# Adaptive-LayerNorm linear attention and Mish block in fp32: Q of two blocks as seven block products, and a new order of the steps around them

## The chip, the cores and the metric

The kernel runs on one core of a Trainium2 chip. A core has a matmul engine (TensorE, PE below), three engines for elementwise work (VectorE or DVE, ScalarE or ACT, GpSimd or POOL), and SyncE (SP), whose queue here only starts DMA transfers; POOL starts some too. Every engine works through a queue of its own in the order in which the program emitted it, and waits on semaphores for the others. The metric is the device time of one execution in microseconds (us), taken as the median over runs.

## The reference, cut to what matters

`x` is 2048 rows of 512, all data is fp32. The hidden width is F = 1792, there are 32 heads of 16, and `c` is one row, so that the six modulation vectors are the same for all rows.

```
mod = silu(c) @ w_mod                         # sa, ca, ga, sb, cb, gb, 512 each
h   = layernorm(x) * (1 + ca) + sa
q, k, v = split(h @ wqkv)                     # wqkv: 512 x 1536
phi(t)  = where(t > 0, t + 1, exp(t)) + 1e-6
kv  = phi(k)^T v   per head                   # 16 x 16
z   = sum over rows of phi(k)
o   = phi(q) kv / (phi(q) . z + 1e-6)
x   = x + ga * (o @ wo)
h   = layernorm(x) * (1 + cb) + sb
x   = x + gb * (mish(h @ w1 + b1) @ w2)
```

## The kernel before, in words

**Tiles.** The rows are four blocks (NB = 4) of 512, each of four row tiles of 128. An fp32 product is made of three fp32r products: `split` (L71) makes of a tile a high part (a copy on ACT) and a low part (a subtraction on DVE), and `mm3` (L65) issues high x high, high x low and low x high. One Q unit, a 128 x 512 output over four contraction steps, is thus 12 matmuls. Almost all SBUF tiles are 512 wide and share one pool of slots; PSUM has eight banks in three tags (`acc` 4, `h` 3, `tp` 1).

**Order.** The order is written out by hand: the order of emission is the order of each engine's queue. Work beside the matmuls lives in generators: `spawn` starts one, and each `tick()` advances all that run by one step. Moving a `spawn` or a `tick` thus moves instructions in the queues of DVE, ACT, POOL and SP relative to those of PE.

**Attention.** For each block `k_unit(b, t)` (L259) makes K of a row tile, with `phi` (L242: exp and relu on ACT, the min and sum `ku` on DVE) and a split. `g_unit(b, t)` (L271) accumulates `gacc`, the normalized x transposed times phi(k), over all rows in four PSUM banks; its operand is the split `xn` (L266) of a row tile. `transpose` (L226) makes the modulated, transposed `hf` and its split `hT`, which K and Q multiply. After the last block, `z_unit` (L280) gives the sums, and the denominators' weights follow from them on DVE (`zs`, `hmask`).

Then comes the Q phase. `q_unit(b, g)` (L288) makes Q, transposed, 128 outputs for the 512 rows of a block, and `phi` on it. `attend(b, wait)` (L683) multiplies phi(q) by the z weights (`den`, on the single `tp` bank), takes the reciprocal on DVE, sends it to DRAM and reads it back spread over partitions (`rd`, four loads on POOL's queue), lets `wait` ticks pass, and then makes `q * rd` and its split `qs`. `kv_ps` and `m_ps` fold kv and wo into one matrix `m`; `o_unit(b, t)` (L726) multiplies `qs` by `m`, and adds the residual on DVE. Before the change the order is: Q of block 0; one unit of block 1; `den` of block 0; `kv_ps`; the rest of block 1; `m_ps`; Q of block 2 with `attend(1, 4)` spawned; `o_unit(0, 0..3)` with `attend(2, 5)` spawned; `norm_sums(0)` (L733, the second LayerNorm's sums) spawned; Q of block 3.

**Second part.** The FFN's first product works on two blocks of rows at once by the Winograd form of Strassen's scheme: seven block products and 15 additions in place of eight products. For a pair `g` of hidden tiles, `pair_begin` (L947), `pair_early` (L963), `pair_middle` (L972) and `pair_end` (L979) issue the products `a11 b11`, `a12 b21`, `s1 t1`, `s2 t2`, `s3 t3`, `a22 t4` and `s4 b22`; partial sums stay in a PSUM bank and are copied to SBUF on ACT as `u1`, `u2`, `u3` (L950, L968, L975) while more is accumulated onto them. `rows(...)` prepares the sums of w1 for a pair: loads on SP, four half-width operations on DVE (L600 to L603), four splits. `two_pairs` (L1001) interleaves the first two pairs, with two functions `between` called inside; the second of them, `trail`, issues `d_unit` (L914), the FFN's second product, of an earlier hidden tile.

Of the kernel before, what the change touches and what calls it, by code (L numbers as in the profile page):

```python
# [13 lines left out]
P = 128  # L14
# [11 lines left out]
def block_kernel(ctx: ExitStack, tc: tile.TileContext, x, wqkv, wo, w1, b1t, w2, c, wmodt, out):  # L26
# [18 lines left out]
    def f32(t):  # L45
        return t.bitcast(F32)
# [3 lines left out]
    def spawn(gen):  # L50
        fresh.append(iter(gen))
# [169 lines left out]
    def sums_shift(key, b, t, sums):  # L221
        dve.tensor_tensor(nb[key, b][:, t:t + 1], sums[:, 0:1], rs[key, b][:, t:t + 1], op=ALU.mult)

    xn, hT, wq, wk = {}, {}, {}, {}

    def transpose(key, b, j, sc0, sh0, ptag, hi_engine=act):  # L226

        p = ps(ptag, f"tp_{key}_{b}_{j}")
        for t in range(4):
            pe.transpose(p[:, P * t:P * (t + 1)], xt[key, b, t][:, P * j:P * (j + 1)], ident)  # L230

        def post():
            hf = sb(f"hf_{key}_{b}_{j}")
            act.activation(hf, p, AF.Identity, bias=mc[:, sh0 + j:sh0 + j + 1], scale=mc[:, sc0 + j:sc0 + j + 1])
            yield from split(f"hT_{key}_{b}_{j}", hf, hT, (key, b, j), hi_engine=hi_engine)

        return post()
# [50 lines left out]
    def q_unit(b, g):  # L288
        p = ps("h", f"pq_{b}_{g}")
        gs = slice(P * g, P * (g + 1))  # L290
        for k in range(4):
            mm3(p, [w[:, gs] for w in wq[k]], hT["x", b, k], k == 0, k == 3)
        pq[b, g] = sb(f"q_{b}_{g}")
        spawn(phi(p, f"q_{b}_{g}", pq[b, g]))

    bc = {}

# [98 lines left out]
    for k in range(4):  # L396
        hi, lo = sb(f"hT_x_0_{k}h", F32R), sb(f"hT_x_0_{k}l", F32R)
        hT["x", 0, k] = hi, lo

        for dst, piece in [(hi, half_) for half_ in ((0, 256), (256, 512))] + [(tp0[k], (0, 512))] if k == 0 else \  # L400
                [(hi, (0, 512)), (tp0[k], (0, 512))]:
            cs = slice(*piece)
            act.activation(dst[:, cs], tp0[k][:, cs], AF.Identity, bias=mc[:, k:k + 1], scale=mc[:, 4 + k:5 + k])
        if k < 3:
            run(split(f"wk_{k + 1}", wraw[1, k + 1], wk, k + 1, pool, pool))
        if k == 0:
            act.preload_act_table_set("exp_and_others")
            mod_pair(1)
        if k == 1:
            step(xsplit[0])  # L410
            mod_col(7, sc_bc)
            plus_one(7, 8)
        if k == 3:
            step(xsplit[0])
        dve.tensor_tensor(lo, tp0[k], f32(hi), op=ALU.subtract)
        if k == 0:
            mod_pair(2)
        if k == 1:
            mod_col(3, sc_bc)
        if k < 2:  # L420
            for t in range(4):
                pe.matmul(kp[t], hi[:, tss[t]], wk[k][0], start=k == 0, stop=False)
            for st, mv_ in (hi, wk[k][1]), (lo, wk[k][0]):
                for t in range(4):
                    pe.matmul(kp[t], st[:, tss[t]], mv_, start=False, stop=False)
        if k == 0:
            tp0.append(ps("acc", "tp_x_0_3"))
            transposes_0(3, tp0[3])
# [211 lines left out]
    for b in range(1, NB):  # L640
        last = b == NB - 1
        if b == NB - 2:
            spawn(mod_side(range(8, 12), 1))
        for t in range(4):
            k_unit(b, t)
            if b + 2 < NB:
                load_x(b + 2, t)
            if last:
                load_wqkv(0, t)
                xn_split(b, t)  # L650
            elif t >= 2:
                xn_split(b, t - 2)
            tick()
        if b + 2 < NB:
            spawn(ln_side(b + 2))
        if last:
            spawn(wo_scale())
        for t in range(4):
            if not last and t % 2 == 0:
                for j in (t, t + 1):  # L660
                    tr = transpose("x", b + 1, j, 4, 0, "tp" if j == t else "h")
                    next(tr)
                    spawn(tr)
# [155 lines left out]
            if k % 2:  # L819
                yield  # L820

    for g in range(4):
        q_unit(0, g)
        load_x(1, g, "r")
        if g == 1:
            spawn(kv_side())
            spawn(mod_side([20, 21, 22, 23, 16, 17, 18, 19], 2))
        if g == 2:
            next(early_rows[0])
        tick()  # L830
    q_unit(1, 0)
    load_x(2, 0, "r")
    tick()
    run(early_rows[0])
    next(early_rows[1])
    attending = attend(0, 5)
    next(attending)
    kvs = {}
    kv_ps = ps("acc", "kv_ps")
    for g in range(4):  # L840
        for k in range(4):
            for j in range(2):
                cs = slice(P * g + 64 * j, P * g + 64 * (j + 1))
                pe.matmul(kv_ps[64 * j:64 * (j + 1), cs], wv[k][:, cs], zs[k][:, cs], start=k == 0, stop=k == 3)
    for j in range(2):
        js = slice(64 * j, 64 * (j + 1))
        dve.tensor_tensor(kv.rearrange("p (g m) -> p g m", g=4)[js, :, js],
                          kv_ps.rearrange("p (g m) -> p g m", g=4)[js, :, js],
                          bmask[js, js].unsqueeze(1).to_broadcast([64, 4, 64]), op=ALU.mult)
    spawn(split("kv", kv, kvs, 0))  # L850
    next(attending)
    spawn(attending)
    for g in range(1, 4):
        q_unit(1, g)
        load_x(2, g, "r")
        tick()
    for g in range(4):
        m_ps = ps("acc", f"m_ps_{g}")
# [1 line left out]
        spawn(split(f"m_{g}", m_ps, ms, g))  # L860
    run(early_rows[1])
    for g in range(4):
        q_unit(2, g)
        if g == 1:
            spawn(attend(1, 4))
            spawn(mod_side(range(12, 16), 1))
        load_x(3, g, "r")
        tick()
    for t in range(4):
        o_unit(0, t)  # L870
        if t == 1:
            spawn(attend(2, 5))
        tick()
    spawn(norm_sums(0))
    for g in range(4):
        q_unit(3, g)
        tick()
    act.preload_act_table_set("mish")

    order = {8: [(0, 0), (0, 2)], 9: [(0, 1)], 10: [(0, 3), (1, 0)], 11: [(1, 2)], 12: [(1, 1)], 13: [(1, 3)]}  # L880
# [95 lines left out]
        add(c22, pc, u3)  # L976
        spawn(later(c22, 2 * g + 1, 1))

    def pair_end(c0, g, pa, pc, u2):  # L979
        c12 = sb(f"c12_{g}")  # L980
        m = mish(product(g, "a22", "t4", onto=pa), c0, 2 * g + 1)
        next(m)
        spawn(m)
        product(g, "s4", "b22", onto=pc)
        add(c12, pc, u2)
        spawn(later(c12, 2 * g, 1))
        tick()

    def pair_unit(c0, g, odd, between):
        begun = pair_begin(c0, g, ("tp" if odd else "h", "h"))  # L990
# [307 lines left out]
```

## Time and profile before

| | us |
|---|---|
| median of 3 runs | 502.73 |
| lowest, highest | 500.97, 503.97 |
| the profiled execution | 502.79 |
| its span, first to last instruction | 501.0 |

Granted TensorE clock over the span: 0.997 of full.

| engine | busy us | share of the span | instructions |
|---|---|---|---|
| PE | 491.8 | 98% | 2652 |
| DVE | 349.7 | 70% | 679 |
| ACT | 289.8 | 58% | 517 |
| POOL | 143.2 | 29% | 246 |

How to read the profile's rows. A row of the timeline gives start and length in us, engine, source line, operation, out<-in by the program's names with buffer numbers left out, partitions x elements, and in brackets how long the engine had been idle and what it waited for. "x32" says that so many instructions are shown as one row. Matmuls are pipelined: their rows overlap, and the distance from start to start is what one costs. The granted clock is the share of full speed that the throttle gave TensorE. The profile is of one execution, so a sum of its durations is made against that execution's own time.

### The profile page before, as it was taken

The numbers are of one execution on the slowest core, as the hardware profiler recorded it, in microseconds if no ns is written. First come the engines' busy times: TensorE is split into PE (matmuls) and PEld (weight loads), VectorE is DVE, ScalarE is ACT, GpSimd is POOL, SyncE is SP. The second block draws the span as 40 slices with busy tenths as digits, with TensorE's granted clock in tenths as the row PEclk, the third lists the DMA queues.
The fourth block names the chain that finished last, engine by engine and source line by source line (L and its number), as shares of the span: only waits on it lengthen the run. The fifth ranks groups of instructions, "written<-read, shape, count | busy, mean of one in ns | idle before, by whom it ended". The sixth has DMA issues, their size and how long they took to land.

```text
span 501.0 us, 7672 instructions
## 1 busy us (share of the span) xinstructions
PE 491.8 (98%) x2652; PEld 414.9 (83%) x2652; DVE 349.7 (70%) x679; ACT 289.8 (58%) x517; POOL 143.2 (29%) x246
## 2 busy tenths in 40 slices
PE   7999999999999999997999999999999999999997
PEld 6788888878878888886888888888788888899997
DVE  6885664869996679956566864679953755559772
ACT  6877684735461979557568646278354555568100
POOL 3473120000212323123034311424465031545200
PEclk9999999999999999998999999999999999999999
DMA  8724754373464307419999945999999352688512
GB/s 305 284 66 88 191 126 98 100 259 106 101 182 124 96 25 254 148 42 359 329 367 314 366 144 195 298 374 324 374 379 268 83 154 84 163 216 233 125 44 85
DMA packets 66765, 98.58 MB, mean 197 GB/s; under 512 B 7405, under 2 KB 31861, under 8 KB 66726
## 3 DMA queue, kind: packets, MB, share of 16 engines
q0 software_dynamic: 29360, 45.31, 32.9%
q1 hardware_dynamic: 37220, 52.51, 32.0%
q8 instruction: 21, 0.34, 0.3%
q10 hardware_dynamic: 146, 0.26, 0.1%
q14 instruction: 18, 0.15, 0.1%
HBM read 62.92 MB, written 33.03 MB: 192 GB/s over the span
## 4 chain that ended last, share of the span: by engine, by line
PE 93%; ACT 4%; DVE 2%; DMA 1%; issue 0%; ACTq 0%
PE p_a L940 18%; PE p_s L940 7%; PE oacc L69 5%; PE oacc L68 5%; PE oacc L67 5%; PE m L69 5%; PE m L68 5%; PE m L67 5%; PE pq L67 3%; PE o L67 3%; PE gacc L68 3%; PE gacc L69 3%; PE o L69 3%; PE gacc L67 3%; PE pq L68 3%; PE o L68 3%
## 5 line engine op out<-in xcount | busy, mean ns | idle before, releaser
L945 DVE TENSOR_TENSOR c<-p_s,u 128x512 f32<-128x512 f32 x28 | 19.4, 691 | 69.2 <-ACT u L975 58.7
L968 ACT ACTIVATE u<-p_a 128x512 f32<-128x512 f32 x12 | 7.2, 599 | 31.1 <-PE p_a L940 31.1
L932 ACT ACTIVATE ub<-c,b1c 128x512 f32<-128x512 f32 x28 | 20.0, 716 | 3.6 <-DVE c L945 3.5
L1198 POOL DMA_DIRECT2D wt_m<-w2t x20 | 14.0, 703 | 25.9 <-PE m L69 17.2
L248 DVE SCALAR_TENSOR_TENSOR ku<-e_k,relu_k 128x512 f32<-128x512 f32 x16 | 11.0, 689 | 14.6 <-ACT relu_k L246 14.6
L796 ACT ACTIVATE hf_n<-tp_n,mc 128x512 f32<-128x512 f32 x16 | 11.7, 769 | 13.4 <-PE tp_n L794 13.4
L192 POOL TENSOR_TENSOR rs_n<-rs_n,half 128x1 f32<-128x1 f32 x16 | 9.6, 604 | 30.7 <-DVE rs_n L218 15.0
L950 ACT ACTIVATE u<-p_a 128x512 f32<-128x512 f32 x14 | 8.3, 596 | 16.7 <-PE p_a L940 16.7
L245 ACT ACTIVATE e_k<-pk 128x512 f32<-128x512 f32 x16 | 9.6, 598 | 13.3 <-PE pk L69 13.2
L245 ACT ACTIVATE e_q<-pq 128x512 f32<-128x512 f32 x16 | 9.4, 589 | 12.7 <-PE pq L69 12.7
L975 ACT ACTIVATE u<-p_a 128x512 f32<-128x512 f32 x14 | 8.3, 594 | 13.0 <-PE p_a L940 13.0
L587 POOL DMA_DIRECT2D w2b<-w2d x20 | 10.6, 550 | 18.1 <-DMA out_dram<-r 5.7
L945 DVE TENSOR_TENSOR c<-p_a,u 128x512 f32<-128x512 f32 x14 | 9.5, 687 | 6.2 <-PE p_a L940 2.7
L695 POOL DMA_DIRECT2D rden_d<-rden x3 | 2.2, 717 | 41.0 <-DVE rden L693 40.8
L192 POOL TENSOR_TENSOR rs_x<-rs_x,half 128x1 f32<-128x1 f32 (+1 forms) x10 | 7.4, 744 | 22.4 <-DVE rs_x L187 21.6
L581 POOL DMA_DIRECT2D wb<-w2d x14 | 9.9, 710 | 13.1 <-PE m L69 8.4
L201 ACT ACTIVATE x<-x,nb_x,rs_x 128x512 f32<-128x512 f32 x15 | 11.5, 810 | 3.6 <-DVE nb_x L196 3.1
L248 DVE SCALAR_TENSOR_TENSOR q<-e_q,relu_q 128x512 f32<-128x512 f32 x16 | 11.0, 687 | 3.4 <-ACT relu_q L246 3.4
L707 DVE SCALAR_TENSOR_TENSOR q<-q,rd 128x512 f32<-128x512 f32 x16 | 10.6, 688 | 3.2 <-DMA rd<-rden_d 3.2
L783 POOL DMA_DIRECT2D nd<-r x8 | 4.6, 571 | 27.7 <-ACT r L201 26.2
L909 ACT ACTIVATE u<-p_a,b1c 128x512 f32<-128x512 f32 x14 | 9.5, 681 | 5.1 <-PE p_a L940 5.1
L719 DVE TENSOR_TENSOR r<-o,r 128x512 f32<-128x512 f32 x16 | 10.8, 678 | 2.3 <-PE o L69 2.3
(1460 smaller groups left out, 1949.2 us busy)
## 6 DMA issues: line engine op xcount, KB each, us to landing
wm<-in_wmodt_dram SPq DMA_DIRECT2D x24, 256.0 KB, 4.6
w2b<-w2d POOLq DMA_DIRECT2D x20, 256.0 KB, 6.6
wt_m<-w2t POOLq DMA_DIRECT2D x20, 256.0 KB, 3.6
r<-in_x_dram SPq DMA_DIRECT2D x16, 256.0 KB, 3.0
x<-in_x_dram SPq DMA_DIRECT2D x15, 256.0 KB, 4.8
w1p<-in_w_dram SPq DMA_DIRECT2D x14, 256.0 KB, 4.5
w2r<-in_w_dram SPq DMA_DIRECT2D x14, 256.0 KB, 3.9
wb<-w2d POOLq DMA_DIRECT2D x14, 256.0 KB, 4.5
```

Of the source, the lines that this page charges most:

```text
L67: pe.matmul(o, st[0], mv[0], start=start, stop=False)
L68: pe.matmul(o, st[0], mv[1], start=False, stop=False)
L69: pe.matmul(o, st[1], mv[0], start=False, stop=stop)
L192: pool.tensor_tensor(y, y, half[:, lo:hi], op=ALU.pow)
L201: act.activation(dst, t, AF.Identity, bias=nb[key, b][:, j:j + 1], scale=rs[key, b][:, j:j + 1])
L245: act.activation(e, p, AF.Exp)
L248: dve.scalar_tensor_tensor(dst, e, 1.0, r, op0=ALU.min, op1=ALU.add)
L796: act.activation(hf[b, j], p, AF.Identity, bias=mc[:, 12 + j:13 + j], scale=mc[:, 16 + j:17 + j])
L932: act.activation(u, p, AF.Mish, bias=b1c[:, f:f + 1])
L940: pe.matmul(p, st, mv, start=onto is None and c == 0 and i == 0, stop=c == 1 and i == 2, skip_group_check=onto is not None)
L945: dve.tensor_tensor(out, p, u, op=ALU.add)
L1198: pool.dma_start(v, w2t[g][:, :, SUM[name], :])
```

## The change

1. Q of blocks 0 and 1 is made as a 2 x 2 block product in the same Winograd form. `q_left` makes the four weight sums of a half of the contraction, `q_right` the four sums and differences of the transposed rows `hf`, both on DVE and with splits; `q_product` issues 6 matmuls; `q_sevens` issues 2 x 7 products with their copies on ACT and six additions `cq` on DVE. The Q weights are loaded one block earlier, and `hf` of blocks 0 and 1 is kept, for block 0 as a tile in SBUF.
2. `q_right` is spawned in blocks 1 and 2 of the K phase, `q_left` in block 2, and `early_rows[0]`, which is `rows(0)`, in block 3 in place of the Q phase.
3. The new order of the Q phase: `q_sevens`; `kv_ps`; `den` of block 0; Q of block 2; `m_ps`; two Q units of block 3; `o_unit(0, 0..3)`; `norm_sums(0)` spawned; the last two Q units. `attend(0, 4)` takes the place of `attend(0, 5)`.
4. In `two_pairs` the tick at the end of the first `pair_end` goes, and so does, for the first two pairs, the tick between. `rows(2, 3)` is spawned earlier, before `o_unit(3, 3)`.

The diff, cut to its core:

```diff
+    def q_left(c):
+        a11, a21, a12, a22 = [wraw[0, k][:, h:h + 256] for k in (c, c + 2) for h in (0, 256)]
+        s12, s34 = sb(f"qs12_{c}"), sb(f"qs34_{c}")
+        s1, s2, s3, s4 = s12[:, 0:256], s12[:, 256:512], s34[:, 0:256], s34[:, 256:512]
+        dve.tensor_tensor(s1, a21, a22, op=ALU.add)
+        dve.tensor_tensor(s2, s1, a11, op=ALU.subtract)
+        dve.tensor_tensor(s3, a11, a21, op=ALU.subtract)
+        dve.tensor_tensor(s4, a12, s2, op=ALU.subtract)
+        yield
+        for n, t in (12, s12), (34, s34):
+            yield from split(f"qs{n}_{c}", t, qa, (n, c))
+
+    def q_right(c):
+        b11, b12, b21, b22 = [hfx.pop((b, k)) for k in (c, c + 2) for b in (0, 1)]
+        t = [sb(f"qt_{c}_{i}") for i in range(4)]
+        for n, (d, u, v) in enumerate(((t[0], b12, b11), (t[1], b22, t[0]), (t[2], b22, b12), (t[3], b21, t[1]))):
+            dve.tensor_tensor(d, u, v, op=ALU.subtract)
+            if n % 2:
+                yield
+        for i in range(4):
+            yield from split(f"qt_{c}_{i}", t[i], qb, (f"t{i + 1}", c))
...
+    def q_sevens(side):
...
+        for o in range(2):
+            pa[o] = q_product(o, "a11", "b11", "h")
+            u1[o] = copy(pa[o], f"qu1_{o}")
+        side(0)
+        for o in range(2):
+            p = q_product(o, "a12", "b21", ("h", "tp")[o])
+            result(0, o, p, u1[o])
+            q_product(o, "s2", "t2", onto=pa[o])
+            u2[o] = copy(pa[o], f"qu2_{o}")
+            side(1 + o)
+        for o in range(2):
+            pc[o] = q_product(o, "s1", "t1", ("h", "acc")[o])
+            q_product(o, "s3", "t3", onto=pa[o])
+            u3[o] = copy(pa[o], f"qu3_{o}")
+            result(1, 2 + o, pc[o], u3[o])
+            side(3 + o)
+        for o in range(2):
+            result(0, 2 + o, q_product(o, "a22", "t4", onto=pa[o]), None)
+        side(5)
+        for o in range(2):
+            q_product(o, "s4", "b22", onto=pc[o])
+            result(1, o, pc[o], u2[o])
+        side(6)
...
             k_unit(b, t)
...
+            if b == NB - 2:
+                load_wqkv(0, t)
+                if t == 1:
+                    spawn(q_right(1))
+            if last and t == 0:
+                spawn(early_rows[0])
             if last:
-                load_wqkv(0, t)
...
             g_unit(b, t)
+            if b == 1 and t == 1:
+                spawn(q_right(0))
+            if b == 2 and t < 2:
+                spawn(q_left(t))
...
-    for g in range(4):
-        q_unit(0, g)
...
-    q_unit(1, 0)
...
+    q_sevens(beside_q)
+    load_x(2, 3, "r")
     next(early_rows[1])
...
-    for g in range(1, 4):
-        q_unit(1, g)
-        load_x(2, g, "r")
+    for g in range(4):
+        q_unit(2, g)
+        if g == 1:
+            spawn(attend(1, 4))
+            spawn(mod_side(range(12, 16), 1))
+        load_x(3, g, "r")
         tick()
...
     run(early_rows[1])
     for g in range(4):
-        q_unit(2, g)
...
-    for t in range(4):
-        o_unit(0, t)
...
-    spawn(norm_sums(0))
-    for g in range(4):
-        q_unit(3, g)
-        tick()
+        q_unit(3, g)
+        tick()
         if g == 1:
+            for t in range(4):
+                o_unit(0, t)
+                if t == 1:
+                    spawn(attend(2, 5))
+                tick()
+            spawn(norm_sums(0))
...
-    def pair_end(c0, g, pa, pc, u2):
+    def pair_end(c0, g, pa, pc, u2, step=True):
...
-        tick()
+        if step:
+            tick()
...
-        pair_end(c0, g0, *s0)
+        pair_end(c0, g0, *s0, step=False)
...
     for t in (2, 3):
+        if t == 3:
+            spawn(rows(2, 3))
         o_unit(NB - 1, t)
         tick()
...
         if g == 1:
-            spawn(rows(2, 3))
             norm_next()
-            two_pairs(0, 0, 1, begun, (tick, trail(0, rows(3, 2))))
+            two_pairs(0, 0, 1, begun, (lambda: None, trail(0, rows(3, 2))))
```

More of the change, by code (lines that the diff above doesn't have):

```diff
@@ new lines, in q_right, with q_product @@
+    def q_right(c):
[7 more added lines that the diff above has]
+            yield from split(f"qt_{c}_{i}", t[i], qb, (f"t{i + 1}", c))
+    def q_product(o, left, right, tag=None, onto=None):
+        p = onto if onto is not None else ps(tag, f"pq_{left}_{o}")
+        for c in range(2):
+            if left[0] == "a":
+                st, lo = wq[c + 2 * (left != "a11")], 256 * (left == "a22") + P * o
+            else:
+                n = int(left[1])
+                st, lo = qa[(12, 12, 34, 34)[n - 1], c], 256 * ((n - 1) % 2) + P * o
+            mv_ = qb[right, c] if right[0] == "t" else hT["x", int(right[2]) - 1, c + 2 * (right[1] == "2")]
+            st = [h[:, lo:lo + P] for h in st]
+            for i, (l, r) in enumerate(((st[0], mv_[0]), (st[0], mv_[1]), (st[1], mv_[0]))):
+                pe.matmul(p, l, r, start=onto is None and c == 0 and i == 0, stop=c == 1 and i == 2,
+                          skip_group_check=onto is not None)
+        return p
@@ new lines, in q_sevens, with result, copy @@
+    def q_sevens(side):
+        pa, pc, u1, u2, u3 = {}, {}, {}, {}, {}
+        def result(b, g, p, u):
+            if u is not None:
+                c = sb(f"cq_{b}_{g}")
+                dve.tensor_tensor(c, p, u, op=ALU.add)
+                p = c
+            pq[b, g] = sb(f"q_{b}_{g}")
+            spawn(phi(p, f"q_{b}_{g}", pq[b, g]))
+        def copy(p, name):
+            u = sb(name)
+            act.activation(u, p, AF.Copy)
+            return u
+        for o in range(2):
[21 more added lines that the diff above has]
+        side(6)
@@ L398, in block_kernel @@
         hT["x", 0, k] = hi, lo
[L400 to L401 removed]
+        hf_k = hfx[0, k] = sb(f"hf_x_0_{k}")
+        for dst, piece in [(hi, half_) for half_ in ((0, 256), (256, 512))] + [(hf_k, (0, 512))] if k == 0 else \
+                [(hi, (0, 512)), (hf_k, (0, 512))]:
             cs = slice(*piece)
@@ L844, in block_kernel @@
                 pe.matmul(kv_ps[64 * j:64 * (j + 1), cs], wv[k][:, cs], zs[k][:, cs], start=k == 0, stop=k == 3)
+    attending = attend(0, 4)
+    next(attending)
+    next(attending)
     for j in range(2):
```

31 lines of the change are left out of this document (12 added, 19 removed).

## The prediction

> **What bounds the kernel now.** I read the first part of the profile's page, then the chain of work that ended last, then the waits of TensorE (PE), and only then stretches of the timeline.
>
> ```profile
> span 501.0 us, 7672 instructions
> ...
> PE 491.8 (98%) x2652; PEld 414.9 (83%) x2652; DVE 349.7 (70%) x679; ACT 289.8 (58%) x517; POOL 143.2 (29%) x246
> ...
> PE 93%; ACT 4%; DVE 2%; DMA 1%; issue 0%; ACTq 0%
> ```
>
> The table of waits begins for PE with this row (total, times, longest, in us):
>
> ```profile
> PE p_a L940 <- ACT u L975: 2.7, 1, 2.7
> ```
>
> PE is busy for 491.8 of 501.0 us and carries 93% of the chain, so a matmul left out is time won, and a wait that reaches PE is time lost. One wait is large, the 2.7 us on the copy `u` of L975. The price of a matmul, and the Q phase, come from these rows: the first Q matmul, and the first of `o_unit(0, 0)` and of `o_unit(0, 1)`, 12 matmuls apart.
>
> ```profile
> 107.59 0.40 PE L67 MATMUL pq<-hT_x_0h,wq_0h 128*128 128x512 f32 x1
> 147.85 0.39 PE L67 MATMUL o<-m_0h,qs_0h 128*128 128x512 f32 x1
> 150.57 0.39 PE L67 MATMUL o<-m_0h,qs_0h 128*128 128x512 f32 x1
> ```
>
> (150.57 - 147.85) / 12 = 0.227 us for one. The other engines are not free everywhere; in this table the columns are the stretch, then busy time and count for PE, PEld, DVE, ACT, POOL, and then granted clock, DMA share and GB/s.
>
> ```profile
> 60.00:72.00 12.00, 12.00 (x58) 10.00 (x57) 5.67 (x12) 8.90 (x16) 2.84 (x4) 1.00 0.55 145
> 72.00:84.00 12.00, 12.00 (x60) 10.02 (x59) 7.48 (x14) 7.97 (x14) 0.86 (x1) 1.00 0.61 132
> 84.00:96.00 12.00, 12.00 (x55) 9.83 (x54) 6.54 (x11) 6.91 (x14) 1.17 (x2) 1.00 0.23 66
> 108.00:120.00 12.00, 12.00 (x54) 9.90 (x54) 11.79 (x33) 5.90 (x11) 0.00 (x0) 1.00 0.42 139
> 120.00:132.00 12.00, 12.00 (x136) 9.67 (x135) 11.88 (x30) 5.95 (x11) 0.73 (x1) 1.00 0.34 91
> 132.00:144.00 12.00, 12.00 (x82) 9.53 (x80) 11.93 (x26) 8.31 (x17) 2.93 (x5) 1.00 0.84 219
> 168.00:180.00 12.00, 12.00 (x81) 9.65 (x80) 8.58 (x18) 11.71 (x23) 1.10 (x2) 1.00 0.14 37
> 230.00:235.00 5.00, 4.55 (x13) 3.63 (x14) 3.81 (x9) 3.20 (x6) 2.06 (x4) 0.67 1.12 380
> ```
>
> From 108 to 144 us, the Q phase, VectorE (DVE) is full: 11.79, 11.88 and 11.93 of 12 us. The change puts DVE work just before this stretch and into it. ScalarE (ACT) is full at 168 to 180.
>
> **What the seven products remove.** Q of blocks 0 and 1 is 2 x 4 units x 12 = 96 matmuls now. Seven products, each for two output halves, with two contraction steps of three passes, are 7 x 2 x 2 x 3 = 84. The 12 left out are worth 12 x 0.227 = -2.7 us.
>
> **What they add on DVE, and where it stands.** Engines take their queues in order, so an added subtraction delays whatever is queued behind it. I place each by the emission order and price it by rows. Four places matter, all waits of PE on something late.
>
> (a) `g_unit(1, 3)`. `q_right(0)` is spawned after `g_unit(1, 1)`, and its four full-width subtractions stand on DVE ahead of `xn_1_3l`.
>
> ```profile
> 55.96 0.66 DVE L81 TENSOR_TENSOR xn_3l<-x,xn_3h 128x512 fp32r<-128x512 f32 x1
> 58.13 0.39 PE L69 MATMUL gacc<-pk_3h,xn_3l 128*128 128x512 f32 x1
> ```
>
> The split ends at 56.62 and PE takes it at 58.13: slack 1.5 us. Rows under (b) show that DVE starts a full-width operation every 0.61 us (75.79 to 76.40); four, dependent in pairs, are about 2.5. PE then waits 1.0 us (0 if DVE has idled before them, 1.2 with more bubbles).
>
> (b) `g_unit(2, 2)` and `g_unit(2, 3)`. Here stand `q_right(1)`, the low splits that `q_right(0)` left over, and `q_left` of both halves.
>
> ```profile
> 64.44 0.69 DVE L248 SCALAR_TENSOR_TENSOR ku<-e_k,relu_k 128x512 f32<-128x512 f32 x1 [4.02 <-ACT relu_k L246]
> 75.79 0.69 DVE L81 TENSOR_TENSOR hT_x_1l<-hf_x,hT_x_1h 128x512 fp32r<-128x512 f32 x1 [0.64 <-ACT hT_x_1h L75]
> 76.40 0.68 DVE L168 SCALAR_TENSOR_TENSOR wm<-wm,sc_row 128x512 f32<-128x512 f32 x1
> 78.82 0.69 DVE L81 TENSOR_TENSOR xn_3l<-x,xn_3h 128x512 fp32r<-128x512 f32 x1
> 81.72 0.39 PE L69 MATMUL gacc<-pk_3h,xn_3l 128*128 128x512 f32 x1
> 133.99 0.42 DVE L600 TENSOR_TENSOR s<-w1p 128x256 f32<-128x256 f32 x1
> 135.46 0.69 DVE L81 TENSOR_TENSOR a_1l<-w1p,a_1h 128x512 fp32r<-128x512 f32 x1
> ```
>
> From `ku_2_0`, which waits for ACT and so can't start earlier, to `xn_2_3l` there are 18 DVE operations before and 36 after. The 36 are 28 of full width (28 x 0.61 = 17.1) and two chains of four half-width ones like that from 133.99 to 135.46 (2 x 1.47 = 2.9). Even without any idle moment the last ends at 64.44 + 20.0 = 84.4, and PE wants it at 81.72: 2.7 us late. With the idle moments that remain (0.64 and the like, twice) it would be 4.0. I take 2.7.
>
> (c) Block 3. `rows(0)` moves here from the Q phase: four half-width and four split operations on DVE (about 3.5 us), its loads on SP, and the Q weights' loads one block earlier. In 60 to 84 us DMA engines are 0.55 and 0.61 busy, so I give the loads no price; if one came late, the cover would be the block that lies between load and use. The DVE part is hidden by DVE's idle time in 84 to 96 us, 12 - 6.54 = 5.5 us; I take zero, and at most 1 if that idle time lies at the wrong moments.
>
> (d) From the Q products to `o_unit(0, 0)`. Seven products need six additions `cq` in the full stretch, and bring two units of block 3's Q ahead of the o units; against that `rows(0)` has left.
>
> ```profile
> 113.96 0.68 DVE L248 SCALAR_TENSOR_TENSOR q<-e_q,relu_q 128x512 f32<-128x512 f32 x1
> 114.56 1.40 DVE L818 SCALAR_TENSOR_TENSOR zs<-gacc,mc,zs 128x512 f32<-128x512 f32 x2
> 121.32 1.26 PE L688 MATMUL den<-q,hmask 128*32 128x128 f32 x32
> 125.63 0.85 DVE L847 TENSOR_TENSOR kv<-kv_ps,bmask 64x256 f32<-64x256 f32 x2
> 126.52 0.35 DVE L692 TENSOR_SCALAR rden<-den,tiny_den 128x128 f32<-128x128 f32 x1
> 145.84 0.95 DVE L693 RECIPROCAL rden<-rden 128x128 f32<-128x128 f32 x1
> 155.68 0.69 DVE L707 SCALAR_TENSOR_TENSOR q<-q,rd 128x512 f32<-128x512 f32 x1 [1.50 <-DMA rd<-rden_d]
> ```
>
> PE, unhindered: before, 147.85 - 107.59 = 40.3 us lie between first Q matmul and first o matmul. After, this holds 156 matmuls of Q in place of 144 (+2.7) and half a `den` group less (-0.6): `o_unit(0, 0)` is due at 150.0, its second matmul, which reads `m_0l`, at 150.25. DVE: the first `cq` takes the place of the row at 113.96. To the end of `q_0_3` there are 15 full-width operations, 6 weight rows at the same 0.61, and two `zs` pairs at 1.40: 15.6 us, plus 1.1 that DVE waits for the copy `u3` of the tenth product (PE gets there at 107.59 + 60 x 0.227 = 121.2). So `q_0_3` ends at 130.7. The last of `den_0` (0.3) and the reciprocal (0.35 + 0.95) bring 132.3. The broadcast back through memory took from 145.84 + 0.95 = 146.8 to 155.68, 8.9 us, in block 2: `rd` lands at 141.2. DVE, with the kv product (0.85), two weight rows, five full-width operations and the next reciprocal, would be there at 138.8; it waits. From there to `m_0l` are 14 full-width operations, two weight rows and five half-width ones: 11.6, so `m_0l` ends at about 152.85, and PE has lost 2.6 us, whether at `den_0`, `den_1` or here. If `rd` landed 2.5 us sooner, DVE would not wait, and it would be near zero; with 0.1 of bubble for ten dependent pairs 3.6. I take 2.6, which is worked out from the nearest landing.
>
> (e) `norm_sums(0)` is spawned after two of block 3's Q units in place of none, with two steps of 12 matmuls fewer (5.4 us) to the transposes that read its last tile.
>
> ```profile
> 178.62 0.82 ACT L201 ACTIVATE n<-r,nb_n,rs_n 128x512 f32<-128x512 f32 x1 [0.20 <-DVE nb_n L222]
> 182.97 1.03 PE L794 MATMUL tp_n<-ident,n 128*128 128x128 f32 x8
> ```
>
> Slack now: 182.97 - 179.44 = 3.5. So up to 5.4 - 3.5 = 1.9 us, on an ACT that has 11.71 of 12 us at work already; I take 1.6, between 0 and 1.9.
>
> **The removed step of the first pairs.** The 2.7 us wait:
>
> ```profile
> 223.27 0.82 ACT L201 ACTIVATE r<-r,nb_n,rs_n 128x512 f32<-128x512 f32 x1 [1.84 <-DVE nb_n L222]
> 227.13 0.61 ACT L75 ACTIVATE w_2h<-w2r 128x512 fp32r<-128x512 f32 x1
> 229.82 0.57 ACT L975 ACTIVATE u<-p_a 128x512 f32<-128x512 f32 x1
> 227.35 0.39 PE L69 MATMUL oacc<-w_0h,a_0l 128*128 128x512 f32 x1
> 230.44 0.50 PE L940 MATMUL p_a<-t_0h,a_1h 128*128 128x512 f32 x1 [2.71 <-ACT u L975]
> ```
>
> PE's matmul of 230.44 was due at 227.58. Without the two steps the five ACT operations from 227.13 on, four splits and a Mish, queue behind the copy, which could start 2.7 earlier. But `rows(2, 3)`, now spawned at the third o unit, puts its four half-width operations (1.47) on DVE ahead of `nb_n`, and ACT's `r` at 223.27 waits for that. So the copy comes at 227.13 + 1.5 = 228.6, PE goes on at 229.25: -1.2 us (-2.8 if `nb_n` isn't held up, 0 if something else is last). Behind the wait PE ran at 0.67 of its clock for 5 us (230 to 235): another 5 x 0.33 = 1.65 us, which I take as gone with a wait of 1.7.
>
> The Trainium skill's page "TensorE: Matmul & The Clock Gate", section "HAM oscillation — how this bites in real kernels", gives as its rule that only idle gaps above about 3.4 us bring the clock down. The trace disagrees: 2.71 us of waiting was followed by the 0.67. By the page none of the waits worked out here would cost clock; by the trace one the size of (b) may. So I add half of 1.65 for (b), +0.8.
>
> **The sum**, against the profiled execution, 502.79 us with a span of 501.0 (1.8 around it, 0.06 above the median of 502.73): -2.7 (matmuls) +1.0 (a) +2.7 (b) +2.6 (d) +1.6 (e) -1.2 -1.65 (first pairs) +0.8 (clock) = +3.15, so 505.9 us. This case's own range: 2.7 at (b) is firm, and with (d) 1.5 lower and (e) 1.2 lower it is 503.2; with the upper ends of (b), (d) and (a) and the rest of (b)'s clock 509.2, and 510.5 if the copy gains nothing: 503 to 510.5.
>
> **Rivals.** *The lateness does not reach PE* (faster). The chain of (a), (b), (d), (e) supposes that DVE and ACT are as late as their queues are long. For it: DVE is only 5.67 and 7.48 of 12 us busy in the stretches of (a) and (b), and (d) and (e) rest on one landing time and one slack. Against it: (b) counts busy time alone. If these four together cost 1.9 us, and the copy comes the full 2.7 earlier, -2.7 - 2.8 - 1.65 + 1.9 gives 497.5. It decides where the new waits come to less than the 5.6 us that matmuls, copy and clock bring. Chance 0.26.
>
> *It cancels.* The old cost goes and the new waits bring about as much: between 3 and 8 us of them in all. The nearest way: PE's lateness at (d) gives ACT the time that it lacks at (e), and (b) costs no clock; then 505.9 - 1.6 - 0.8 = 503.5, inside the 0.5% or 2.5 us that is about what a measurement of this kernel can tell from no change. For it: (e)'s slack is counted from PE's end, not ACT's. Against it: ACT has no room there. Chance 0.19.
>
> *Clock after every wait* (slower still, within my 0.55). If (b), (d) and the remaining 1.7 us wait each bring a stretch like 230 to 235, and (b) comes at 4.0: 505.9 + 0.8 + 1.65 + 1.65 + 1.3 = 511.3. Chance 0.13 of the 0.55. That the change does not do what it says can be left out: the queue order has 12 matmuls fewer and the copy five places earlier.
>
> **Numbers.** Likeliest, at 0.55: slower, 505.9. Range 497 to 510.5: it goes down to the faster rival and up to nearly the clock case, with about 0.2 left out at the two ends together. Faster by over 0.5% 0.26, within it 0.19, slower 0.55.
>
> **What would show it.** In the profile after: 12 PE rows fewer, and a Q stretch of 84 back-to-back matmuls; among PE's waits `gacc` on `xn_3l` or `xn_2l` near 58 and 80 us with 1 and 2.7; waits of `den`, or `o` on `m_0l`, summing to 2.6; `tp_n` on ACT's `n`; the wait on `u` at the first pairs at 1.7 and a clock of 1.00 behind it. If `gacc` waits nowhere in block 2, (b) is wrong and with it the sign.

## The result, and the profile after

The changed kernel takes 515.16 us (median of 4 runs, 514.84 to 516.07) against 502.52 us for the kernel before (4 runs, 500.97 to 503.97): 1.0255 times as long, 95% interval 1.0221 to 1.0289. The forecast had the sign, 505.9 us was 9 us too low, and the range ended at 510.5. The profiled execution took 515.32 us, its span is 513.6 us.

The page of the changed kernel begins so (engine, busy us, share, instructions; then the chain that ended last):

```profile
span 513.6 us, 7722 instructions
...
PE 493.6 (96%) x2640; PEld 413.5 (81%) x2640; DVE 368.9 (72%) x713; ACT 298.4 (58%) x535; POOL 144.5 (28%) x246
...
PE 71%; DVE 11%; ACT 8%; issue 5%; DMA 3%; POOL 0%; ACTq 0%; POOLq 0%; DVEq 0%
```

PE has the 12 rows fewer, but its share of the chain fell from 93% to 71%: DVE, ACT and DMA have taken over places in it. Which, the waits of PE say (total, times, longest, us):

```profile
PE m L69 <- DVE a_11l L81: 2.4, 1, 2.4
PE tp_n L889 <- ACT n L201: 2.2, 1, 2.2
PE o L67 <- DVE m_0l L81: 1.9, 1, 1.9
PE gacc L69 <- DVE xn_2l L81: 1.9, 1, 1.9
PE gacc L69 <- DVE xn_3l L81: 1.8, 2, 0.9
PE p_a L1031 <- ACT u L1066: 1.5, 1, 1.5
...
PE den L783 <- DVE q L250: 0.8, 2, 0.7
```

The first line is a wait of which the prediction said nothing; the next five are its (e), (d), (b), (a) with (b), and the first pairs. Behind two of the waits the clock fell. Windows of the changed kernel (the clock is the third number from the end):

```profile
160.00:165.00 5.00, 5.00 (x16) 3.92 (x16) 5.00 (x11) 1.77 (x4) 0.00 (x0) 0.66 0.16 28
190.00:195.00 5.00, 2.78 (x15) 2.29 (x14) 4.79 (x16) 3.77 (x8) 1.52 (x3) 0.92 0.13 43
195.00:200.00 5.00, 5.00 (x20) 3.95 (x20) 2.21 (x6) 5.00 (x10) 0.89 (x2) 0.74 0.48 177
235.00:240.00 5.00, 5.00 (x23) 3.80 (x21) 2.57 (x7) 2.96 (x5) 0.59 (x1) 1.00 1.04 365
```

The same matmuls in the two timelines, start in us, tell where the 12.6 us of span came from:

| matmul | before | after | later by |
|---|---|---|---|
| first with `xn_1_3l` | 58.13 | 59.56 | 1.4 |
| last of the K phase | 106.90 | 112.54 | 5.6 |
| first of Q | 107.59 | 113.23 | 5.6 |
| first of `o_unit(0, 0)` | 147.85 | 159.71 | 11.9 |
| first of the FFN (`p_a`) | 202.96 | 215.23 | 12.3 |
| first `oacc` with `w2b` | 330.58 | 340.55 | 10.0 |
| last `m` | 497.29 | 509.92 | 12.6 |

So block 2 of the K phase lost 4.2 us, the stretch up to the first o unit 6.2, of which 2.2 is work that was moved there, the rest up to the FFN 0.4 although 4.9 us of work had left it, the first pairs gained 2.3, and something in the last stage lost 2.6.

### The profile page after: what moved, and what is told of

The parts are those of the page before. It is cut to its first block, busy times and chain, and to the rows that moved or that the text cites. A ratio compares the mean times of both kernels' runs of the same rounds, so it can differ in the third digit from the quotient of the medians.

```text
span 513.6 us, 7722 instructions
## 1 busy us (share of the span) xinstructions
PE 493.6 (96%) x2640; PEld 413.5 (81%) x2640; DVE 368.9 (72%) x713; ACT 298.4 (58%) x535; POOL 144.5 (28%) x246
## 4 chain that ended last, share of the span: by engine, by line
PE 71%; DVE 11%; ACT 8%; issue 5%; DMA 3%; POOL 0%; ACTq 0%; POOLq 0%; DVEq 0%
PE p_a L1031 17%; PE p_s L1031 7%; PE oacc L69 5%; PE oacc L67 5%; PE oacc L68 5%; PE m L69 5%; PE m L68 5%; PE m L67 5%; PE o L67 2%; PE o L69 2%; PE o L68 2%; PE gacc L69 2%; PE gacc L68 2%; ACT x L201 1%; PE gacc L67 1%
## 5 line engine op out<-in xcount | busy, mean ns | idle before, releaser
L247 ACT ACTIVATE e_k<-pk 128x512 f32<-128x512 f32 x16 | 9.5, 594 | 11.9 <-PE pk L69 11.9
L259 POOL DMA_DIRECT2D ku<-ku x8 | 7.1, 893 | 18.6 <-DVE ku L250 17.9
```

## The experiments

Medians stand against the kernel before run on the same chip, 502.6 to 502.9 us. The changed kernel's own ratio has the interval 1.0221 to 1.0289. Where that of a run overlaps it (experiments 6 to 9, 12 and 13), the time alone can't tell the two apart for certain, and the argument rests on the waits in the profile.

**1. Part 4 of the change alone: the step dropped in both calls of `two_pairs`, `rows(2, 3)` earlier.**

```diff
 kernel before
-        pair_end(c0, g0, *s0)
+        pair_end(c0, g0, *s0, step=False)
...
+        if t == 3:
+            spawn(rows(2, 3))
...
-            two_pairs(0, 0, 1, begun, (tick, trail(0, rows(3, 2))))
+            two_pairs(0, 0, 1, begun, (lambda: None, trail(0, rows(3, 2))))
```

> The kernel before with part 4 of the change alone (the dropped steps in the two interleaved pairs, and the earlier rows(2, 3)). The function with the dropped step is called twice, for the first pairs of blocks 0 and 1 and again for the first pairs of blocks 2 and 3. Theory: the first call wins 2.3 us (wait on u3 1.5 instead of 2.7, no clock loss), the second loses 2.4 us, because an addition that waits for the copy u3 now stands on VectorE ahead of the low half of a_11: 502.5 - 2.3 + 2.4 = 502.6 us. Rival (the late wait comes from something else, such as the order of the Q phase): the first gain alone, 500.2 us.

504.44 us, ratio 1.0032 (1.0020 to 1.0044). The late wait is there, without any of the other parts. The time is 1.8 above the expected, and most of that is a low-clock stretch behind that wait, which the profile of the changed kernel did not have: in this one (505.29 us) the window 380 to 385 us ran at 0.78. The three of ten executions with a mean clock of 0.999 or 1.0 took 502.92 to 503.68 us.

**2. The same, with the step kept in the second call.**

```diff
 experiment 1
-        pair_end(c0, g0, *s0, step=False)
+        pair_end(c0, g0, *s0, step=c0 > 0)
```

> The kernel before with part 4 of the change, but the step is dropped in the first call only and kept in the second. Theory: 502.5 - 2.3 = 500.2 us, with no wait on a_11l. Rival (the gain at the first pairs in the changed kernel came from the later arrival there, not from the dropped steps): 502.5 us.

500.49 us, ratio 0.9952 (0.9937 to 0.9967). This is the version that beats both kernels, the one before by 0.5%. Its waits of PE begin so:

```profile
PE p_a L940 <- ACT u L975: 1.5, 1, 1.5
PE warm L129 <- POOL ones L123: 1.1, 1, 1.1
PE tp_x L378 <- ACT x L201: 1.0, 2, 0.6
```

**3. The changed kernel with the step kept in the second call.** The same edit on the changed kernel.

> The changed kernel with the step kept in the second call of the interleaved pairs. Theory: 515.2 - 2.4 = 512.8 us, and PE has no wait on a_11l any more. Rival: the wait stays near 390 us and the time at 515.2.

512.01 us, ratio 1.0184 (1.0164 to 1.0203): 3 us back, and the wait on `a_11l` is gone. The DVE rows show what the missing tick did, first before the change, then after it:

```profile
375.14 0.69 DVE L945 TENSOR_TENSOR c<-p_s,u 128x512 f32<-128x512 f32 x1 [0.88 <-PE p_s L940]
375.75 0.68 DVE L81 TENSOR_TENSOR a_12l<-u,a_12h 128x512 fp32r<-128x512 f32 x1
376.35 0.68 DVE L81 TENSOR_TENSOR a_11l<-u,a_11h 128x512 fp32r<-128x512 f32 x1
378.59 0.69 DVE L945 TENSOR_TENSOR c<-p_s,u 128x512 f32<-128x512 f32 x1 [1.56 <-ACT u L975]
```

```profile
385.13 0.69 DVE L1036 TENSOR_TENSOR c<-p_s,u 128x512 f32<-128x512 f32 x1 [0.88 <-PE p_s L1031]
388.57 0.69 DVE L1036 TENSOR_TENSOR c<-p_s,u 128x512 f32<-128x512 f32 x1 [2.76 <-ACT u L1066]
389.18 0.68 DVE L81 TENSOR_TENSOR a_12l<-u,a_12h 128x512 fp32r<-128x512 f32 x1
389.78 0.69 DVE L81 TENSOR_TENSOR a_11l<-u,a_11h 128x512 fp32r<-128x512 f32 x1
```

Before, the two low halves ran in the 3 us in which DVE would otherwise wait for the copy `u`; after, the addition that waits stands ahead of them, and PE is waiting for the second one, `a_11l`.

**4. The changed kernel with plain Q.**

```diff
 changed kernel, without the spawns of q_right and q_left
-    q_sevens(beside_q)
+    for n in range(8):
+        q_unit(n // 4, n % 4)
+        if n < 7:
+            beside_q(n)
```

> The changed kernel with Q of blocks 0 and 1 as 8 x 12 plain matmuls again, no q_left and q_right, everything else as changed (order, loads, rows(0) in block 3, pairs). Theory (VectorE's queue is late by the added sums, splits and additions): 12 matmuls cost 2.7 us, the waits in blocks 1 and 2 of the K phase go (5.3 us), so do the waits up to the first o unit (4) and the low clock behind them (1.75); the waits on ACT's n and on a_11l stay: 515.2 + 2.7 - 11 = 506.9 us. Rival (loads and rows(0) moved into blocks 2 and 3 make the waits of block 2): they stay, and the time is about 511 us.

511.93 us, ratio 1.0181 (1.0164 to 1.0198): a miss for both theories. The waits in blocks 1 and 2 are gone, so those belong to the sums and their splits, not to the moved loads or to `rows(0)`; 515.2 + 2.7 for the matmuls - 5.3 for these waits is 512.6, near what was measured. That is near the rival's 511 too, but its waits in block 2 did not stay. And PE still waits 2.5 us for `m_0l`, without one `cq` in the queue, and DVE is idle for more than half of the time before it:

```profile
125.00:130.00 5.00, 5.00 (x33) 3.94 (x33) 1.05 (x3) 1.80 (x4) 0.00 (x0) 1.00 0.34 95
130.00:135.00 5.00, 5.00 (x102) 4.34 (x98) 2.13 (x5) 0.95 (x3) 0.57 (x1) 1.00 0.58 170
135.00:140.00 5.00, 4.64 (x50) 3.48 (x49) 3.95 (x10) 2.82 (x6) 2.29 (x5) 1.00 0.17 54
140.00:145.00 5.00, 5.00 (x22) 4.12 (x23) 2.35 (x4) 1.60 (x3) 0.79 (x2) 1.00 0.86 220
```

```profile
133.18 0.95 DVE L782 RECIPROCAL rden<-rden 128x128 f32<-128x128 f32 x1
145.13 0.69 DVE L796 SCALAR_TENSOR_TENSOR q<-q,rd 128x512 f32<-128x512 f32 x1 [2.71 <-DMA rd<-rden_d]
155.60 0.69 DVE L81 TENSOR_TENSOR m_0l<-m_ps,m_0h 128x512 fp32r<-128x512 f32 x1
```

It is the new order: the round trip of `rden` starts only after all of Q of blocks 0 and 1 (before the change 60 Q matmuls came ahead of it, here 96), 72 Q matmuls instead of 84 lie between it and the o unit, and DVE has work queued behind its landing. From the first Q matmul (107.74) to the first of the o unit (156.34) PE took 48.6 us in place of 40.3; of the 8.3 us more, 4.9 are matmuls moved there, so that the order alone lost about 3.5, against 4.0 in the changed kernel.

**5. The sums on POOL.**

```diff
 changed kernel, in q_left and q_right
-            dve.tensor_tensor(d, u, v, op=ALU.subtract)
+            pool.tensor_tensor(d, u, v, op=ALU.subtract)
... (the same for the four operations in q_left)
```

> The changed kernel with the sums of q_left and q_right (8 full-width, 8 half-width subtractions or additions) on POOL in place of VectorE; their splits stay. POOL needs 1.3 us for a full-width one of the same kind at the start of the profile and is idle for most of 50 to 125 us. Theory (a and b are VectorE's queue): from ku_2_0 to xn_2_3l VectorE has 24 operations instead of 36, 14.6 us, and ends at about 79 against 81.7 wanted, so the waits of gacc on xn go, 5.3 us: 515.2 - 5.3 = 509.9. Rival (the low splits and their waits for ScalarE are enough to be late, or POOL's LayerNorm steps behind the sums come late): at most half of it, 512.5 or more.

520.11 us, ratio 1.0335 (1.0304 to 1.0367), slower still, and not for either reason. Three rows of POOL, then DVE's beside them:

```profile
53.19 1.63 POOL L318 TENSOR_TENSOR qt<-hf_x,qt 128x512 f32<-128x512 f32 x1
54.78 1.72 POOL L318 TENSOR_TENSOR qt<-hf_x,hf_x 128x512 f32<-128x512 f32 x1
56.48 1.71 POOL L318 TENSOR_TENSOR qt<-hf_x,qt 128x512 f32<-128x512 f32 x1
```

```profile
53.59 1.78 DVE L81 TENSOR_TENSOR hT_x_1l<-hf_x,hT_x_1h 128x512 fp32r<-128x512 f32 x1
55.30 1.76 DVE L83 SCALAR_TENSOR_TENSOR pk_3l<-ku,pk_3h 128x512 fp32r<-128x512 f32 x1
56.98 0.68 DVE L183 BATCH_NORM_STATS2 st_x<-x 128x6 f32<-128x512 f32 x1
```

While POOL subtracts, a DVE operation with two inputs takes 1.76 to 1.78 us in place of 0.69; the one with a single input keeps its 0.68. PE waits 2.7 us in block 1 and 2.2 and 2.3 in block 2.

**6. `rows(1)` later.**

```diff
 changed kernel
-    run(early_rows[1])
...
             spawn(norm_sums(0))
+            spawn(early_rows[1])
```

> The changed kernel with the second half of rows(1) (four half-width operations and four splits on VectorE, 3.65 us) moved from before block 3's Q to a generator spawned behind o_unit(0, 3). Theory A (the wait of o on m_0l is VectorE's work that is queued between the landing of rd and m_0l): m_0l comes 3.65 us earlier, the wait of 1.9 us and the low clock behind it (1.75) go: 515.2 - 4 = 511.2. Theory B (the round trip den, DRAM, rd alone sets it, and VectorE has time): no change, 515.2.

513.76 us, ratio 1.0213 (1.0188 to 1.0237). No wait on `m_0l` is left, so theory A has the mechanism: what is queued between the landing and `m_0l` counts. Its time, 511.2, was missed, since the first transposes now wait 3.6 us for ACT's `n` in place of 2.2: `rows(1)` also has four copies on ACT, which here stand among the sums ahead of that `n`.

**7. The transposes later.** In the table of transposes by o unit, (0, 0) and (0, 2) go from unit 8 to 9, the others close up behind.

> The changed kernel with the first transposes of the normalized rows one o unit (12 matmuls, 2.7 us) later. Theory (they wait for ScalarE, which is behind with the sums and n of block 0): the wait of 2.2 us and the low clock behind it (1.4) go: 515.2 - 4 = 511.2. Rival (ScalarE is so far behind that whatever comes first in its place waits): the wait only moves, 514 or more.

513.14 us, ratio 1.0216 (1.0184 to 1.0248). Half and half: the wait on `n` is gone, and 1.4 us come back one unit later as a wait of a transpose for ACT's `hf_n`.

**8. All four repairs.**

> The changed kernel with all four repairs: sums on POOL, the rest of rows(1) later, transposes one unit later, and the step kept in the second call of the interleaved pairs. If the seven products only cost what their neighbours' lateness costs, 515.2 - 5.3 - 4 - 4 - 2.7 = 499.2 us, below the kernel before (502.6) and about 1.3 below the kernel before with the first pairs' steps alone (500.5); waits of den of some 1.2 us stay. If the repairs share their gain (each takes cover that another needs), 503 to 506.

513.70 us, ratio 1.0217 (1.0188 to 1.0245), a miss for both values. The waits on `m_0l`, on `n` and on `a_11l` are gone, but `gacc` waits 5.1 and 2.3 us for DVE's low halves in blocks 1 and 2, as in experiment 5: POOL's cost ate the rest.

**9. The sums later in the K phase.**

```diff
 changed kernel
-                if t == 1:
-                    spawn(q_right(1))
...
-            if b == 1 and t == 1:
+            if b == 1 and t == 3:
                 spawn(q_right(0))
-            if b == 2 and t < 2:
-                spawn(q_left(t))
+            if b == 2 and t > 1:
+                spawn(q_left(t - 2))
+            if b == 2 and t == 3:
+                spawn(q_right(1))
```

> The changed kernel with q_right(0) spawned two row tiles later (after g_unit(1, 3)), q_left after g_unit(2, 2) and (2, 3), and q_right(1) after g_unit(2, 3); rows(0) stays in block 3. Theory (the waits of blocks 1 and 2 are VectorE's queue): from ku_2_0 to xn_2_3l stand 22 operations instead of 36, so the waits of gacc on xn in blocks 1 and 2 go (5.3 us); but from there to the z sums stand 51 instead of 35, 43 of full and 8 of half width, 29 us against the 26.3 that the kernel before takes, so 1 to 3 us come back as new waits in block 3: 511 to 513. Rival (the sums delay ScalarE's copies wherever they stand, not by their count): as late as now, 515.

512.88 us, ratio 1.0218 (1.0192 to 1.0244), as the count of operations said. The waits of blocks 1 and 2 are gone, and two come back in block 3:

```profile
PE gacc L68 <- DVE pk_2l L83: 0.7, 1, 0.7
...
PE z L286 <- DVE ku L257: 0.4, 1, 0.4
```

Q begins at 110.53 in place of 113.23.

**10. Seven products with later sums, `rows(0)` and `rows(1)` among the o units, later transposes and the step kept.** The edits of 3, 7 and 9, and:

```diff
 changed kernel
-            if last and t == 0:
-                spawn(early_rows[0])
...
-    next(early_rows[1])
+    next(early_rows[0])
...
-    run(early_rows[1])
+    next(early_rows[1])
...
                 if t == 1:
                     spawn(attend(2, 5))
+                if t in (0, 3):
+                    spawn(early_rows[t // 3])
```

> The same later sums, with the step kept in the second call of the pairs, the transposes one o unit later, and rows(0) and rows(1), their loads and VectorE work, moved behind o_unit(0, 0) and o_unit(0, 3). Theory (every loss is VectorE work, or ScalarE work behind it, queued ahead of something due): block 3 has 43 operations, 26 us, and no wait; m_0l comes 3.65 us earlier and the wait at o_unit(0, 0) goes; the wait of the transposes is half its size: 512.0 (with the step kept) - 5.3 - 4 - 2 = 500.7. Rival (the order of the Q phase itself, den later and the o units among block 3's Q, costs by its DMA round trip and by ScalarE's sums): 504 to 507.

506.29 us, ratio 1.0082 (1.0060 to 1.0103): the rival's value. All the added waits of the K phase and the one on `m_0l` are gone. The first o unit begins at 152.29, 4.4 us behind experiment 2, of which 2.2 is moved work. The waits that are left lie in the Q phase and behind it, but for the first pairs':

```profile
PE o L69 <- DVE qs_2l L81: 2.5, 1, 2.5
PE p_a L1031 <- ACT u L1066: 1.5, 1, 1.5
...
PE den L781 <- DVE q L250: 0.9, 2, 0.7
PE o L67 <- ACT qs_2h L75: 0.6, 1, 0.6
```

The longest of them is neither the round trip through DRAM nor ACT's sums, which the rival names: the low half `qs_2l` stood on DVE behind a reciprocal, a residual addition and its statistics. In this profile the clock behind it fell for 6 us (185 to 190 at 0.68, 190 to 195 at 0.64).

**11. `rows(2, 3)` where it was, with experiment 2's steps.**

> The kernel before with the steps dropped at the first pairs only, as in e2_pairs_first (500.5), but rows(2, 3) spawned where the kernel before has it. Theory (the 1.5 us that PE still waits for the copy u3 is the four half-width operations ahead of nb_n on VectorE): they now stand behind nb_n, ScalarE's r comes 1.5 us earlier, the wait shrinks to 0.1: 499.0. Rival (the copy waits for something else that is last next): 500.5.

503.49 us, ratio 1.0023 (1.0007 to 1.0039). A miss for both: the wait for the copy is gone, as the theory has it, and a longer one has taken its place, since the halves of the next pair now come too late:

```profile
PE p_a L940 <- DVE a_2l L81: 3.3, 1, 3.3
```

The profiled execution (501.78 us) is the fastest of twelve, with a mean clock of 0.999; ten of the others had 0.993 to 0.996.

**12. Extra matmuls in one wait.**

```diff
 changed kernel
         if g == 1:
+            fill = ps("tp", "fill")
+            for i in range(8):
+                pe.matmul(fill, wq[0][0][:, 0:P], hT["x", 3, 0][0], start=i == 0, stop=i == 7)
             for t in range(4):
                 o_unit(0, t)
```

> The changed kernel with 8 extra matmuls (128x512, operands long at hand, result not read) in front of o_unit(0, 0), where PE waits 1.9 us for m_0l: 8 x 0.227 = 1.8 us of work in the wait. Theory (the low clock behind a wait comes from PE's idleness in it): no stretch of low clock behind the wait, o_unit(0, 0) begins at the same time, and the kernel is 1.7 us faster: 513.5. Rival (the low clock there has another reason, such as the load of the matmuls that follow): the clock falls as before, 515.2, or 517 if the extra matmuls add their own time.

515.99 us, ratio 1.0272 (1.0246 to 1.0298). The profiled execution (514.33 us) is as the theory has it, full clock behind the filled wait, where the changed kernel had 0.66:

```profile
160.00:165.00 5.00, 4.75 (x21) 3.90 (x22) 5.00 (x11) 2.31 (x5) 0.00 (x0) 1.00 0.17 44
```

Its mean granted clock is 0.996, against 0.993. But the other three had 0.990, lower than the changed kernel, so that the time settles nothing.

**13. Extra matmuls in two waits.** Eight more ahead of the transposes of unit 8.

> The changed kernel with 8 extra matmuls of 0.227 us in front of o_unit(0, 0) and 8 more in front of the first transposes of the normalized rows, the two waits (1.9 and 2.2 us) behind which the changed kernel's profile shows the low clock. Theory (a low stretch follows idleness of PE that is over about 1.9 us, in some executions and not in others): both stretches go, the mean granted clock is 0.997 to 1.0 in most executions in place of 0.993, and the time is 512 us (515.2 - 3.3) with no more than the extra matmuls' own overhang on top. Rival (the low stretch moves to another of the five waits whatever is filled): clock 0.993 or below as before, 515 to 516.

513.83 us, ratio 1.0214 (1.0190 to 1.0238), 1.3 below the changed kernel, less than half of the hoped-for 3.2. Six executions: two at clock 1.0 (512.13 and 512.75 us), one at 0.997 (513.6), three at 0.992 and 0.993 (514.06 to 514.95). The profiled one is of the last kind. Both filled waits have full clock behind them; behind two that were not filled, of 1.9 and 2.4 us, it fell:

```profile
85.00:90.00 5.00, 5.00 (x16) 3.85 (x15) 5.00 (x11) 1.92 (x4) 0.00 (x0) 0.66 0.36 104
160.00:165.00 5.00, 4.47 (x20) 3.34 (x19) 5.00 (x10) 2.85 (x6) 0.00 (x0) 1.00 0.44 112
195.00:200.00 5.00, 5.00 (x26) 4.14 (x25) 3.83 (x9) 5.00 (x9) 1.90 (x4) 1.00 0.57 212
390.00:395.00 5.00, 5.00 (x20) 4.16 (x20) 0.62 (x2) 1.32 (x2) 1.66 (x4) 0.77 0.14 21
```

So idleness of PE makes a stretch possible and does not make it certain: in the changed kernel's own profile the waits of 1.9 (at 83 us) and 2.4 us (at 390) went without. The rival, that the stretch moves elsewhere, fits the clock of three of the six executions and not that of the two at 1.0.

## Why the prediction was right or wrong

**Matmuls**: right. 2640 rows against 2652, and the moved work adds up to -2.7 us.

**(a)**: right, 1.1 us against 1.0. PE's matmul of 59.56 waited 0.93 us. (The other 0.35 us at that point were there from the start of the K phase.)

**(b)**: the mechanism is right, shown by experiments 4 and 9; the size was taken at the bare busy time, 2.7, and came out at 4.2, a little above the upper bound. What was mis-sized is the idle time that remains: the named waits took 2.05 and 1.03 us more than a step, and the rest was lost in small ones ahead of them. DVE needed 21.05 us for the same 36 operations (from `ku` at 66.13 to the end of `xn_3l` at 87.18), where the count gave 20.0. The half stretch of low clock that went with (b), +0.8, did not come in the profiled execution.

**(c)**: right. With `rows(0)` in block 3 and the sums away from blocks 1 and 2, experiment 4 has no wait in blocks 1 to 3 that the kernel before did not have.

**(d)**: 4.0 us against 2.6 (11.9 - 5.6 = 6.2, less the moved 2.2), a little above its upper bound of 3.6. Moved by the 5.6 us by which Q begins later, its own times hold up to the landing: reciprocal done at 137.9, landing at 146.8; the trace has 138.2 and 146.4. Behind that DVE needed 13.2 us to the end of `m_0l` in place of 11.6, mostly because it waited a second time, for another part of `rd`, which the sum took as one landing:

```profile
146.43 0.69 DVE L802 SCALAR_TENSOR_TENSOR q<-q,rd 128x512 f32<-128x512 f32 x1 [0.54 <-DMA rd<-rden_d]
148.29 0.69 DVE L802 SCALAR_TENSOR_TENSOR q<-q,rd 128x512 f32<-128x512 f32 x1 [1.17 <-DMA rd<-rden_d]
```

The cause was put down to too much at once. The prediction wrote the loss to DVE's queue and the landing together; experiment 4 shows that the order alone, without the additions, brings the wait on `m_0l`, and experiment 6 that it is the work queued behind the landing that turns the late landing into a wait. The additions bring the waits of `den` on `q`, 0.8 us, which experiment 4 doesn't have.

**(e)**: the place and the tile that PE waits for are right; the wait was 2.2 us (2.5 with the restart) against 1.6, and its upper bound, 1.9, was too low, because it came from moving slack alone. ACT, which the prediction named, is part of the cause: its sums run there almost without a gap from 176.5 to 191.8 us, four more copies among them lengthen the wait (experiment 6), and with the wait away part of it appears at ACT's next product (experiment 7). But the `n` that came last was held up by DVE:

```profile
188.60 0.15 DVE L218 TENSOR_SCALAR rs_n<-sums_n 128x1 f32<-128x1 f32 x1 [0.72 <-ACT scrap_n L214]
189.05 0.95 DVE L788 RECIPROCAL rden<-rden 128x128 f32<-128x128 f32 x1
192.80 0.22 DVE L222 TENSOR_TENSOR nb_n<-sums_n,rs_n 128x1 f32<-128x1 f32 x2
192.98 2.22 ACT L201 ACTIVATE n<-r,nb_n,rs_n 128x512 f32<-128x512 f32 x3 [1.20 <-DVE nb_n L222]
```

Between `rs_n` and `nb_n` DVE is full for 4.2 us, with the reciprocal, a residual addition, its statistics and two low halves, and ACT stands idle for the last 1.20 us of it, where before the change it waited 0.20. The longest wait of experiment 10, on `qs_2l`, is DVE's too.

**First pairs**: the wait was 1.5 us against the predicted 1.7, with full clock behind it (235 to 240 us at 1.00), and the gain at that place 2.3 us against 2.85. Alone, in experiment 2, it is 2.2.

**The step that failed outright** is in the sentence that priced the removed step: it followed the first call of `two_pairs` and not the second. The argument `step=False` holds for both. In the second call the missing tick costs 2.65 us (12.63 - 9.97 at the last and the first matmuls around it), which no term had. Experiments 1, 2 and 3 show it alone and taken back.

**The clock** is the other large one. It was counted at half a stretch, for (b) alone, and the rule in the text, that a wait "the size of (b) may" cost one, was applied to no other. The profile has stretches behind the waits of 1.9 us at (d) and 2.2 us at (e), together some 3 us, and none behind (b): in the first, 12 matmuls take 4.44 us in place of 2.72, 1.7 more. By the Trainium skill's page "TensorE: Matmul & The Clock Gate", section "What's actually happening", the activity window runs freely, so that the moment of a change varies from one execution to the next. That agrees with experiment 13, whose executions of one program have mean clocks from 0.992 over 0.997 to 1.0. The rule that the prediction cites from the section "HAM oscillation — how this bites in real kernels" of this page of the Trainium skill, that idle gaps of over about 3.4 us are the danger, is too lax for this kernel: 1.9 us were enough in the changed kernel and again in experiment 13. The 3.3 us in experiment 11's profile left the clock at 1.00, but that profile is of one of its two executions without a loss of clock.

Together, above the forecast +3.15 us: second call 2.65, clock 2.2, (b) 1.5, (d) 1.4, (e) 0.9, first pairs 0.55, the start 0.35: 9.5, of the measured 12.5 - 3.15 = 9.4 in the profiled execution. With the second call alone in the sum, the forecast would have been 508.6.

Of the rivals, the one that came nearest is "clock after every wait", at 511.3, in part by luck: of the three stretches that it counts, behind (b), (d) and the first pairs, the profile has only that behind (d), and one behind (e) instead. The two that let the waits cancel or not reach PE did not come near. What speaks against the change as a whole is in experiment 10: with the other losses repaired or reduced it is still slower than before by 0.8%, and 5.8 us above experiment 2, which leaves Q alone. The seven products bring all results of block 0 near the end, so `den` comes later; that the order of the Q phase must follow from that is argued, and one with seven products and no wait was not found and so is not excluded.

## What to carry to other kernels

Where PE is 98% busy, an edit is worth its matmuls only if each engine that feeds PE has room at that place: count its instructions between two points that the trace fixes, and take the bare busy time as the lower bound of the delay, not as its value. Before pricing a change inside a function, list all of its calls: here the win at the first (2.2 us) was taken back at the second. In these profiles every stretch of low clock amid matmuls came behind a wait of 1.9 to 3.2 us, and not every such wait had one, so that a new wait of that size has, besides its own length, a chance of about 1.7 us of low clock. And a chain through memory such as `rden` needs its cover counted anew when the order of the phase changes.

## What the runs showed of the hardware

A POOL subtraction of 128x512 took 1.6 to 1.7 us and stretched a DVE operation with two inputs beside it from 0.69 us to between 1.69 and 1.78, while a DVE operation with one input kept its 0.68. The Trainium skill's page "SBUF — State Buffer", section "Who interferes with whom", says this of two-input DVE instructions beside a GpSimd instruction that reads SBUF; the rows agree.

The granted clock fell in whole stretches: about eight matmuls at 0.43 us a step in place of 0.227 (160.04 to 163.42 us in the changed kernel), which cost 1.6 to 1.7 us, or 0.0033 of the mean clock over 500 us; in experiment 10's profile one was twice as long. By their mean clocks, the six executions of experiment 13 had none, one or two of them, and their times lie up to 2.8 us apart.
